# The P V product of a thresholded attention in four 64x64 tiles and two phases, and the ninth-token blocks transposed by two 64-row transfers

## The chip, the core and the metric

One Trainium2 chip, of which one core is used. The metric is the device time of one execution in microseconds (us); the median of 3 runs of the kernel before is 466.98 us (466.92 to 468.55).

## What is computed

Batch 8, 8 heads, 576 tokens, head dimension 64; then a feed-forward layer of 512 to 768 to 512 on the 8 x 576 tokens. All inputs and the output are float32.

```python
scores = scale * np.matmul(q, k.transpose(0, 1, 3, 2))
thresh = np.max(scores, axis=-1, keepdims=True) - tau
scores = np.where(scores >= thresh, scores, -1000000000.0)
attn = np.exp(scores - np.max(scores, axis=-1, keepdims=True))
attn = attn / (np.sum(attn, axis=-1, keepdims=True) + 1e-09)
attn_out = np.matmul(attn, v)                      # P V
x = attn_out.transpose(0, 2, 1, 3).reshape(B * S, H * D)
h = np.maximum(np.maximum(x @ w1, x @ w2), x @ w3)
out = h @ w_out
```

## The kernel before

**Units.** Four heads of a batch make a quad; there are 16 quads, two for each batch. In a quad, heads 2r and 2r+1 form pair r, and inside a pair the head is i. A token sits at partition p, column c of nine (token = 9p + c), so the 576 tokens of a head are eight blocks of 64 tokens that go in couples of 128, and a ninth block of 64. A chunk is 128 query rows by the 576 keys of one head for each of the two pairs: nine chunks for each quad. Chunk index 4 (`idx == 4`) is the ninth-token block: its first 64 partitions belong to head i = 0 and its last 64 to head i = 1.

**Stages of a chunk.** `scores` (S) makes four float32 matmuls of 64 contraction rows for one r; `maximum` (m) is on VectorE; `exponents` (e) on ScalarE; `numerators` (n on ScalarE, k on VectorE); `reciprocals` (r) on VectorE; `normalized` (p) on GpSimd writes P, 128 x 1152 in bf16; `turned` (t) has SyncE (SP) issue one DMA transpose of P into the quad's tile `ptq`, 128 keys x 9 blocks x 1152 queries.

**The product** (`product`, letter O). For one quad and one r, the output tile `o` holds head i on partitions 64i to 64i+63 and the 576 queries along the free side, in two PSUM banks of 512 and 64 columns. Five steps m accumulate: m = 0 to 3 are four couples of 128 keys, with weights `vb`; m = 4 is the ninth block, with weights `vrb`. The ninth block's 64 keys of pair r lie on partitions 64r to 64r+63 only, so `vrb` is 128 partitions tall and zero elsewhere (six memsets at the start, and `cast_v` fills it in two copies of 64 partitions). Each step is, for the 512 columns and then for the 64, one matmul for each i: 128 contraction rows by 64 output columns of the array, which the trace writes as form `128*64`. That is 20 matmuls and 20 weight loads for each product. `on_scalar` (x) and `on_vector` (w) copy `o` into `xt`: for r = 0 VectorE takes all 576 columns, for r = 1 ScalarE takes 512 and VectorE 64.

**The last batch** (b = 7) is worked in two parts: queries of four couples (256 for each head), then the remaining 320. A product of part 1 is ten matmuls of 256 columns, one of part 2 is ten of 256 and ten of 64. So there are 28 whole products and 8 of parts, 680 matmuls.

**Feed-forward.** `ffn` makes pieces: hidden (`ph`, letter F) and output (`po`). They use `halves`: the contraction of 128 is split over the two 64-row halves of the array (form `64*128`), each half accumulating into its own bank; the letter B issues the second phase, in which the halves swap banks. Ahead of the second phase stands a `tensor.nop()` that waits for the last matmul of the first.

**Order.** The string `ORDER` fixes the order of issue on every engine; each letter makes one step, and `_Ordered` chains each engine's instructions in that order (so nearly every line of the profile is L89). A digit behind S, T, O or F is the PSUM slot, of which there are four of two banks each. T is the transposition of q or k on TensorE (`tp`); l issues loads on SP, y is `cast_v` on GpSimd, o issues stores on SP. PE, SP and GpSimd take their work strictly in that order; there is no other scheduling.

The tile pools that matter: `pt` has 2 buffers, `pp` (P) 6.

Of the kernel before, what the change touches and what calls it, by code (L numbers as in the profile page):

```python
# [12 lines left out]
BF16 = mybir.dt.bfloat16  # L13
AX = mybir.AxisListType.X
AF = bass_rust.ActivationFunctionType
# [22 lines left out]
ORDER = """  # L38
lllS0lmyS1eyS2lmlS3kelmnS0lmegS1repmgS2kyemnS3pT0meS1tmeymaS3S2knS0llremplekT3pnlrS1meqmnpmteprceT2qketS3pS0
anT1rmS2lpnmS3qlempntrcS2pekT1eptS0mnqmelprkalS3petS1mnS2qrmnS0lperlmpetkpeT3mnlS1pmetS2mpnremptekyS0nS2qmlT  # L40
1nzrcaemT1pS3ekpteS0mnS2yrmqelcplnS3rplnmS1tpemS2epmS0tepmS1nrS3mptekpT0erlekO2qtamnpS0melpmleS1kteT3rmnpS0l
nqmleprwnS1qeS2pmtnS0mpeO1czntrmnpS3wekT0permT2aptkeS0pxS3rcnS1gpmtnS2rpmepmetS0mqnO3qmegprnS2wynS0mS1etprmO
3epkeztxS2mewmpF3egS0kpeS2rnBmzF1tmhnkyS3egS2rpmBeF0pnvpBtemF1nkT3zBevF2akS0pghBmnF3tS1rvepBmnpS2F0rveqtS1mp
BmS3ezremF2pghkS1zetBmnF0vS3epgBnmF2pS1vetBmT0hS3rcpeF1S2rmpBmpteF0vpeBknS3ztF1nmS2vyeT3gzBmlO0hrlpalnpF1wle
T3ytBcnS0kS2nlmzO3nlrmeqlvelS2pS0rwxrmyF1npmS3gqBekqeF2vntpBmnS0pS1hmpgeS2mpeS3rmpeF0tmpeBrnS1pvS2tepmF0nzS3
metBrmpT2nS1vpaS3tnS0zmS2ermtpF1nkpnmS3eByrtmepkepF2lemlukS0utkBermnpoT1rekpoS0ecO3lupmtnpO1weoqurktpnS3T0xr
wS2mapoF1meT3qlS0cetBqmF3phS2kleqBmlF1nyF0lrnvBelpBrvS3yhpS2mnF1ptmS0epBmeF2ptvnF3BkeS1tvBnS0mhF2rmepS3rBepm
S1nytvF0peS3mpBnlmS2yetvT3eF1maS0lkBeqlS3mhlF2rmeplT1nlcpS0eBlrmpF1tnS3kpeBmnlO0qvernvtpT2S3wapS1nrmF2ptnS0m
qBempF3hS1kqteO2meykT0rxrBwpceS2yvnS0ylmF1nlS3pmelF2pmtBeBkpeS0vhlS3nrtmF1pS2mepBrlmeF3ptS0vepS2mnBtmF1evnT2
lS0kuS3lakS1onF2rmpemlepS0rkepBtmnpmF3erqktepT1uBuconqroS0yuS2pumoS1pT3mteS0ympeO2koayntmO3ewqelrkS1qxlT2wS0  # L50
rnmlpF3mlepcS1BleyF0tmphS2kpeBlmF3nF1lyveBtrknBpS0vhS2lpnrmF3S1pmetBpmeS0veS1tF2mnS3meBlmnF1F0lveBrelkpS2lBh
mF3npF1vBetkS0nrrBvpF2mhpS3BeptmS1nyvT0T3nrmO2parcyetpS0ewqS3mnO1pmeptkeS2qT3xwS0mayF1meqF3kBeqBrnvT2pS0hclS
1ynmtF3nS2mpBelmpF1elS0vetBmnF3rS2veplBmnpF1S0rhkptBemF3nprS2vleBpmS0tnpvF1emS3tuS2rkepS1nrF0mopnmepS3tmeS2p
rmBeptmeykS1yelS2mupS3lumO1temekT0oeF2ronwplakT3nT1qcS0nBpmnqtraS3peO1mqukuqonT0wS3rocpxS2lmeF0ptrF1mepBkpS3
thBremS0plvF2eptS3mS1ymeBlmF0pelS3veBmF2thS1keBknF0lmF3nlBveBlrknF2plS1rhvBnpmF3nS0pvtBepmF2rS1vtepBmpF0hT3k
tBerS2pavS1npF3mS0qmteBrmepO2vnpeS1twnS3mS0nF2meS1meBrmF0phS3knpBemO2eqvterkpT1xT0wS3caF2pnmT1qBtnrcF0pnvS3q
lBempF1lhS2rkyleBtmF0pvS3epBlrnmS1ypnvF2pterS3mpuS0meS2ptF1meymetS3knS0keBomnrmS2eplS3umpF0luroemptS2ekpT1em
T3oBakteqcT1nS2klaS3rmulpO1umoqeorkyeS0S2npmO3nprtwepmS1xpT0wtnmF2qS3ecpBlermF0qlhkS1pteBmnF2S3pvleBymlnF1vS
0eBtnmF2hS3keBlrmpF1nlvF0pnBlrpS2etvBynmS3S1hlrpmF2erpS0mteBpmeS3pvtnF0S1myeyF2pmeBktBeF3khT1vBaS2vnT0qS1rmp
O3meqcepS2wnF0tS1rnmpT3nmBpS2arvpS1temF3qeO0mpeketT2kxBnwS1clF0hrlmS2pnlBrkyeF3lmF1BrveqlBkpnF0lS2vhlBprmT3t  # L60
S1pvaS2pmeF0tS3mpeBkpteF1vnS2pmulS0moS1eF3metrmepS2knpS1S0nmBertmpekpS1nF2mertmpeS0kepS1mBuuqmtnS0keO3omeoku
O1urkoperowT2xpwT0cS3aqtS1nmF2qrF0myepBekS3yBhmF1pnS2vqteBmpnT0F3rcpelS2vBpnlS0mtphS1meS3mteF2knBmleS0lrnvpS
1ermF2plnS3pmteBpmF1eS0rveptBmnpF2kS3htBemF1nS0rvpleBmpF2nlrS3vpelT0mBtpaS1khS3qtmS0eqO2nmekerS3mpS1nmpO0ewt
ermpF2xwT3kpeF0cnBF1ntvT3BnkBarvS2phT3rrF0mqS1pceBmqtT3nS2pvS1ampS0eF3mpteF2mqeBkByeT1vhS0cT3pS2amF1qtnmF3qe
BkqBevS0nrF2vpT1rmupS3noS2cpnS0mpF1etmyeyrmpS2etkBepmnS3ktuS0urmF2peompnorS1kpeS3tmeS0BpmemteS1kuS0urS3kopnO
2ormepeO1pmnpweO0twrxmO2pxkS1eptS0xmnF3mS2teBkF0hmF1nBkS3ervF2peBmpBveS0ytF3hmS1F2emBkF0eBrvnpBrF1vphS3kpBtF
2mF0pveBytS3nyvO1kO2xrmF1xpBrkepS2BhmF3nptF0vepBF1ntvBS2hBmF3vS0eBrmpF1F2vpeBnS3thS0mBmF1eS3veBmnF0vO2urkepo
O1S0xpS3mF1tmekS0eBmweF3rkpnkuS2pnBorrmupteF0pF1hF2nopvF0tuvpF1rhF2pvF0tvF1phF2vF0tvF1hF2uvF0ovF3hoF1vF2vF0h
F3vF1vO2uoO0wF3xF1F2hF0vF1vF2hF0vF1vF2hF0vF1vF2hF0vF1vF2hF0vF1vF2hF0vBvF1uuooBF2uuouoo
"""  # L70


# [28 lines left out]
def kernel(  # L101
# [23 lines left out]
    tensor, scalar, vector, pool, sync = (  # L125
        _Ordered(tc, e) for e in (nc.tensor, nc.scalar, nc.vector, nc.gpsimd, nc.sync))
    B, H, S, D = q.shape
# [8 lines left out]
    one = ctx.enter_context(tc.tile_pool(name="one", bufs=1))  # L136
# [40 lines left out]
    def bank(name, where):  # L177
        return ps_s.tile([128, 1024], F32, name=name, tag=f"s{where}")
# [35 lines left out]
            yield  # L214


    vrs = [one.tile([128, 4, D], BF16, name=f"vr{x}") for x in range(3)]

    def cast_v(L):
        L["vb"] = vp.tile([128, 4, 4, D], BF16, name="vb")  # L220
        pool.tensor_copy(out=L["vb"], in_=L["vm"])
        yield
        L["vrb"] = vrs[(2 * L["b"] + L["qd"]) % 3]
        for r in range(2):
            rows = slice(64 * r, 64 * r + 64)
            pool.tensor_copy(out=L["vrb"][rows, 2 * r:2 * r + 2], in_=L["vr"][rows])
            yield

    def couple(L, n, r, j, rows=slice(0, 128)):

# [121 lines left out]
    def turned(c):  # L352
        L = Ls[c["g"]]
        if "pt" not in L:
            L["pt"] = pt_pool.tile([128, 9, W], BF16, name="ptq")
        sync.dma_start_transpose(out=L["pt"][:, :, c["idx"] * 128:(c["idx"] + 1) * 128], in_=c["P"])

    def product(L, r, target, part=None):

        pt, vb, vrb = L["pt"], L["vb"], L["vrb"]  # L360
        st = {}

        runs = {None: ((0, 640, 0, 512), (512, 576, 512, 64)),
                1: ((0, 640, 0, 256),),
                2: ((256, 896, 0, 256), (512, 576, 256, 64))}[part]

        order = [(m, run) for m in range(5) for run in runs] if part is None else \
            [(m, run) for run in runs for m in range(5)]

        def first(where):  # L370
            st["ps"] = ps = bank("o", where)
            for m, (*q0, p0, n) in order:
                for i in range(2):
                    w = vb[:, 2 * r + i, (1, 3, 0, 2)[m], :] if m < 4 else vrb[:, 2 * r + i, :]
                    tensor.matmul(ps[64 * i:64 * i + 64, p0:p0 + n], w,
                                  pt[:, 4 if m == 4 else m + 5 * r, q0[i]:q0[i] + n],
                                  start=(m == 0), stop=(m == 4))

        def on_vector():
            ps = st["ps"]  # L380
            dst = target(L["b"])[:, 2 * L["qd"] + r, :]
            if part is None and r == 0:
                vector.tensor_copy(out=dst, in_=ps[:, 0:S])
            elif part is None:
                vector.tensor_copy(out=dst[:, 512:S], in_=ps[:, 512:S])
            else:
                vector.tensor_copy(out=dst[:, 256:S], in_=ps[:, 0:320])

        def on_scalar():
            ps = st["ps"]  # L390
            dst = target(L["b"])[:, 2 * L["qd"] + r, :]
            if part is None:
                scalar.activation(out=dst[:, 0:512], in_=ps[:, 0:512], func=AF.Copy)
            elif part == 1:
                scalar.activation(out=dst[:, 0:256], in_=ps[:, 0:256], func=AF.Copy)
            else:
                scalar.activation(out=dst[:, 256:S], in_=ps[:, 0:320], func=AF.Copy)
        p = _Piece((L["b"], L["qd"], r, part), first)
        p.vector = on_vector if part is None or part == 2 and r == 0 else None
        p.scalar = on_scalar if part == 1 or r == 1 else None  # L400
        return p
# [137 lines left out]
        return hTs[b]  # L539

    wl = list(weight_loads())
    for t in vrs:
        for x in range(2):
            vector.memset(t[64 - 64 * x:128 - 64 * x, 2 * x:2 * x + 2, :], 0.0)
    warm = bank("warm", 3)
    for _ in range(WARM):
        tensor.transpose(warm[:, 0:128], identf, identf)
# [2 lines left out]
    for x, (r, n) in enumerate(((0, "q"), (0, "k"), (1, "q"), (1, "k"))):  # L550
        p = transposed(Ls[0], n, r)
# [30 lines left out]
        while True:  # L582
            yield from fn(line[what].pop(0))

    made, pending = [], []
    todo = dict(S=((c, r) for c in chunks() for r in range(2)),
                T=((g, n, r) for g in range(1, NQ) for r in range(2) for n in "qk"),
                O=products(), F=pieces())
# [7 lines left out]
    def issue(what, where):  # L596
        if what == "S":
            c, r = next(todo["S"])
            c[r] = scores(Ls[c["g"]], c["idx"], r, where)
            line["m"].append((c, r))  # L600
        elif what == "T":
            g, n, r = next(todo["T"])
            p = transposed(Ls[g], n, r)
            p.first(where)
            line["a" if n == "q" else "c"].append((p, g, r))
        elif what == "O":
            p = next(todo["O"])
            p.first(where)
            for k, fn in (("x", p.scalar), ("w", p.vector)):
                if fn:  # L610
                    line[k].append(fn)
        elif what == "F":
            p = next(todo["F"])
# [5 lines left out]
        elif what == "B":  # L619
            p = pending.pop(0)  # L620
            p.second()
            line[p.kind].extend(p.done)
        elif what == "m":
            c, r = line["m"].pop(0)
            c["bias", r] = maximum(c, r)
            line["e"].append((c, r))
        elif what == "e":
            c, r = line["e"].pop(0)
# [71 lines left out]
```

## Time and profile before

| | us |
|---|---|
| median of 3 runs | 466.98 (466.92 to 468.55) |
| the profiled execution, first to last instruction (span) | 465.6 |
| median less span | 1.4 |
| PE busy (matmuls) | 437.9 (94%) |
| VectorE, ScalarE, GpSimd busy | 403.9 (87%), 394.0 (85%), 318.7 (68%) |
| PE busy on the P V product | 47.2, in 680 matmuls |
| mean granted TensorE clock | 0.970 |

The page gives no time of its own for the profiled execution beside the span; the 1.4 us between span and median lie around the program's instructions. Busy time of PE counts a matmul to its modelled end, so a PE that is 94% busy still has room between matmuls. The chain is followed back from the last instruction, and its shares say what set the end. A form such as `64*128 64x288` reads: 64 contraction rows by 128 output columns of the array are used, and the moving operand is 64 partitions x 288 columns.

The 36 products in the order of the program, with their start in the trace of before, and the letters that PE sees around them after the change (P is the new letter; digits left out):

| no. | start, us | PE's letters from its O on | no. | start, us | PE's letters |
|---|---|---|---|---|---|
| 1 | 49.78 | O S P S | 17 | 259.11 | O S P S |
| 2 | 59.20 | O S P T | 18 | 265.23 | O T P T |
| 3 | 66.82 | O S P S | 19 | 286.99 | O S P S |
| 4 | 69.89 | O P S | 20 | 289.52 | O P S |
| 5 | 98.15 | O F P T | 21 | 310.74 | O S P F |
| 6 | 101.80 | O S P S | 22 | 316.13 | O T P B |
| 7, 8 | 123.97 | O O P P S | 23, 24 | 338.08 | O O P P T |
| 9 | 149.58 | O T P S | 25 | 362.54 | O S P S |
| 10 | 154.81 | O T P B | 26 | 365.06 | O P F |
| 11, 12 | 176.80 | O O P P S | 27, 28 | 393.73 | O O P P O |
| 13 | 200.04 | O S P S | 29, 30 (part 1) | behind 28 | O P, O P S |
| 14 | 208.31 | O S P T | 31, 32 (part 1) | 411.51 | O O P P F |
| 15 | 231.03 | O T P F | 33, 34 (part 2) | 425.37 | O O S P P S |
| 16 | 237.08 | O T P S | 35, 36 (part 2) | 442.93 | O O P P F |

### The profile page before, as it was taken

The numbers are of one execution on the slowest core, as the hardware profiler recorded it, in microseconds if no ns is written. First come the engines' busy times: TensorE is split into PE (matmuls) and PEld (weight loads), VectorE is DVE, ScalarE is ACT, GpSimd is POOL, SyncE is SP. The second block draws the span as 40 slices with busy tenths as digits, with TensorE's granted clock in tenths as the row PEclk, the third lists the DMA queues.
The fourth block names the chain that finished last, engine by engine and source line by source line (L and its number), as shares of the span: only waits on it lengthen the run. The fifth ranks groups of instructions, "written<-read, shape, count | busy, mean of one in ns | idle before, by whom it ended". The sixth has DMA issues, their size and how long they took to land.

```text
span 465.6 us, 14101 instructions
## 1 busy us (share of the span) xinstructions
PE 437.9 (94%) x5188; PEld 314.1 (67%) x5188; DVE 403.9 (87%) x1115; ACT 394.0 (85%) x794; POOL 318.7 (68%) x416
## 2 busy tenths in 40 slices
PE   7778788999999999979999999999999999999995
PEld 5444545666686777648678676877776777787872
DVE  3987899889999989949999899999999999887641
ACT  3998999789999998849988999988999989866622
POOL 3699788699878878556685687767776597462500
PEclk8995899999999999979999999999999999999999
DMA  8999999799999999996999699999979949654702
GB/s 256 242 210 232 199 222 246 166 237 275 216 232 183 212 161 230 221 215 135 207 214 229 130 189 212 212 196 220 160 190 224 153 84 223 105 102 66 173 32 103
DMA packets 212773, 87.44 MB, mean 188 GB/s; under 512 B 185824, under 2 KB 199648, under 8 KB 212704
## 3 DMA queue, kind: packets, MB, share of 16 engines
q1 hardware_dynamic: 212144, 85.95, 89.6%
q8 instruction: 41, 0.67, 0.6%
q10 hardware_dynamic: 560, 0.59, 0.5%
q14 instruction: 28, 0.23, 0.1%
HBM read 34.60 MB, written 9.44 MB: 95 GB/s over the span
## 4 chain that ended last, share of the span: by engine, by line
PE 70%; DVE 11%; ACT 11%; issue 5%; DMA 2%; POOL 0%; SPq 0%; ACTq 0%; DVEq 0%; POOLq 0%
PE sc L89 25%; PE ph L89 25%; ACT z L89 9%; PE po L89 8%; PE o L89 8%; DVE z L89 6%; PE tp L89 3%; DVE unused L89 2%; DMA ptq<-P 1%; DMA qm<-in_q_dram 1%; DVE kt L89 1%; DVE hT L89 1%; ACT xt L89 1%; ACT hm L89 1%; DVE hm L89 1%
## 5 line engine op out<-in xcount | busy, mean ns | idle before, releaser
L89 POOL TENSOR_SCALAR P<-z,rs 128x576 bf16<-128x576 f32 x288 | 229.5, 810 | 94.7 <-DVE rs L89 58.5
L89 PE MATMUL sc<-kt,qt 64*128 64x320 f32 (+2 forms) x640 | 192.7, 442 | 4.2 <-ACT z L89 2.2
L89 PE MATMUL sc<-kt,qs 64*128 64x256 f32 (+2 forms) x640 | 189.7, 431 | 6.2 <-ACT z L89 4.1
L89 PE MATMUL ph<-xt,w 64*128 64x288 bf16 (+2 forms) x2160 | 170.9, 283 | 1.2 <-DVE xt L89 0.3
L89 PEld LDWEIGHTS <-w 64*128 64x128 bf16 (+1 forms) x2160 | 125.0, 94 | 41.1 <-issue 12.6
L89 ACT ACTIVATE z<-sc,nm 128x576 f32<-128x576 f32 x179 | 129.9, 739 | 21.1 <-DVE unused L89 15.5
L89 DVE TENSOR_SCALAR_CACHE_REDUCE unused<-sc 128x576 bf16<-128x576 f32 x179 | 132.2, 749 | 8.2 <-PE sc L89 7.0
L89 ACT ACTIVATE z<-z 128x576 f32<-128x576 f32 x179 | 121.3, 680 | 0.3
L89 PEld LDWEIGHTS sc<-kt,qs 64*128 64x128 f32 (+1 forms) x640 | 93.2, 182 | 27.3 <-ACT z L89 7.4
L89 PEld LDWEIGHTS sc<-kt,qt 64*128 64x128 f32 (+1 forms) x640 | 93.1, 182 | 18.2 <-ACT z L89 6.7
L89 DVE SCALAR_TENSOR_TENSOR z<-z 128x576 f32<-128x576 f32 x109 | 93.3, 861 | 1.0 <-ACT z L89 0.9
L89 DVE TENSOR_SCALAR_CACHE_REDUCE z<-sc 128x576 f32<-128x576 f32 x109 | 81.1, 750 | 11.7 <-PE sc L89 9.9
L89 ACT ACTIVATE z<-z,nm 128x576 f32<-128x576 f32 x109 | 82.0, 771 | 9.8 <-DVE z L89 9.7
L89 POOL COPY qs<-qt 64x640 f32<-64x640 f32 (+1 forms) x62 | 46.9, 756 | 21.8 <-ACT qt L89 18.6
L89 PE MATMUL po<-wo,hT 64*128 64x512 bf16 (+1 forms) x480 | 54.2, 356 | 0.1
L89 ACT ACTIVATE hm<-ph 128x576 bf16<-128x576 f32 (+2 forms) x54 | 32.1, 595 | 16.2 <-PE ph L89 15.9
L89 DVE TENSOR_TENSOR hm<-ph,hm 128x576 bf16<-128x576 f32 (+2 forms) x54 | 36.9, 684 | 9.9 <-PE ph L89 9.1
L89 PE MATMUL o<-ptq,vb 128*64 128x64 bf16 (+2 forms) x544 | 40.6, 288 | 3.4 <-DMA ptq<-P 3.1
L89 PEld LDWEIGHTS <-hT 64*128 64x128 bf16 (+1 forms) x480 | 30.2, 97 | 17.6 <-issue 3.9
L89 DVE TENSOR_TENSOR hT<-ph,hm 128x576 bf16<-128x576 f32 (+2 forms) x54 | 37.0, 685 | 2.9 <-PE ph L89 1.4
L89 PEld LDWEIGHTS <-vb 128*64 128x64 bf16 x544 | 22.9, 113 | 20.9 <-issue 8.5
L89 ACT ACTIVATION_READ_ACCUMULATOR z<-z 128x1 f32 x179 | 35.4, 198 | 0.0
(32 smaller groups left out, 279.9 us busy)
## 6 DMA issues: line engine op xcount, KB each, us to landing
vm<-in_v_dram SPq DMA_DIRECT2D x32, 256.0 KB, 4.4
out_dram<-ob SPq DMA_DIRECT2D x32, 256.0 KB, 2.7
qm<-in_q_dram SPq DMA_DIRECT2D x15, 512.0 KB, 4.4
km<-in_k_dram SPq DMA_DIRECT2D x15, 512.0 KB, 5.5
stage<-in_moe_w_dram SPq DMA_DIRECT2D x9, 512.0 KB, 4.5
ptq<-P SPq DMA_TRANSPOSE x144, 3.9
stage<-in_moe_w_out_dram SPq DMA_DIRECT2D x3, 512.0 KB, 5.9
qm<-in_q_dram SPq DMA_DIRECT2D x16, 64.0 KB, 2.4
```

What stands on the lines that cost most here:

```text
L89: ins = fn(*a, **kw)
```

## The change

The product uses the array as four tiles of 64x64: the contraction of 128 keys is split into halves h (form `64*64`), and each half accumulates half of the queries into its own bank. In phase 0 half h works on bank 1 - h; in phase 1, behind a `tensor.nop()` that waits for the last matmul of phase 0, the banks are swapped. A whole product is 2 phases of 18 matmuls of 288 columns: four for each of m = 0 to 3, and for m = 4 the two of the half h = r, where the ninth block's keys lie. Parts have 2 x 18 matmuls of 128 or 160 columns. Phase 0 stays at the letter O; phase 1 is issued by a new letter P, of which 36 are put into `ORDER`. Nothing else of `ORDER` is altered. Copies out of `o` keep their engines and sizes, as 2 x 288, 2 x 256 and 2 x 32 columns.

The transposition of chunk 4 becomes two DMA transposes of 64 rows of P, so that each head's 576 queries lie side by side in `ptq`. `vrb` has no zeros left: the six memsets are gone, and `cast_v` fills it with one copy of 128 partitions in place of two of 64.

```diff
-1nzrcaemT1pS3ekpteS0mnS2yrmqelcplnS3rplnmS1tpemS2epmS0tepmS1nrS3mptekpT0erlekO2qtamnpS0melpmleS1kteT3rmnpS0l
+1nzrcaemT1pS3ekpteS0mnS2yrmqelcplnS3rplnmS1tpemS2epmS0tepmS1nrS3mptekpT0erlekO2qtamnpS0PmelpmleS1kteT3rmnpS0
...
-    vrs = [one.tile([128, 4, D], BF16, name=f"vr{x}") for x in range(3)]
+    vrs = [one.tile([128, 2, D], BF16, name=f"vr{x}") for x in range(3)]
...
-        for r in range(2):
-            rows = slice(64 * r, 64 * r + 64)
-            pool.tensor_copy(out=L["vrb"][rows, 2 * r:2 * r + 2], in_=L["vr"][rows])
-            yield
+        pool.tensor_copy(out=L["vrb"], in_=L["vr"])
+        yield
+        yield
...
-        sync.dma_start_transpose(out=L["pt"][:, :, c["idx"] * 128:(c["idx"] + 1) * 128], in_=c["P"])
+        x = c["idx"]
+        for i in range(2) if x == 4 else (None,):
+            rows = slice(0, 128) if i is None else slice(64 * i, 64 * i + 64)
+            at = 128 * x - 64 * (x > 4) if i is None else S * i + 512
+            sync.dma_start_transpose(out=L["pt"][:, :, at:at + rows.stop - rows.start], in_=c["P"][rows])
...
-        runs = {None: ((0, 640, 0, 512), (512, 576, 512, 64)),
-                1: ((0, 640, 0, 256),),
-                2: ((256, 896, 0, 256), (512, 576, 256, 64))}[part]
...
+        pt, vb, vr = L["pt"], L["vb"], L["vrb"]
+        t0, n = {None: (0, S // 2), 1: (0, 128), 2: (256, 160)}[part]
+
+        def phase(swap):
+            ps = st["ps"]
+            if swap:
+                gate = tensor.nop()
+                tc.add_manual_dep(gate.ins, st["last"], ...)
+            for m in range(5):
+                for i in range(2):
+                    for h in (1, 0):
+                        if m == 4 and h != r:
+                            continue
+                        rows = slice(64 * h, 64 * h + 64)
+                        w = vb[rows, 2 * r + i, (1, 3, 0, 2)[m], :] if m < 4 else vr[rows, i, :]
+                        last = (3, 4)[h == r]
+                        a = (1 - h) ^ swap
+                        cols = S * i + t0 + a * n
+                        ins = tensor.matmul(ps[64 * i:64 * i + 64, 512 * a:512 * a + n], w,
+                                            pt[rows, 4 if m == 4 else m + 5 * r, cols:cols + n],
+                                            start=(not swap and m == 0), stop=(swap == 1 and m == last))
+            st["last"] = ins.ins.name
...
-                    tensor.matmul(ps[64 * i:64 * i + 64, p0:p0 + n], w,
-                                  pt[:, 4 if m == 4 else m + 5 * r, q0[i]:q0[i] + n],
-                                  start=(m == 0), stop=(m == 4))
...
-    for t in vrs:
-        for x in range(2):
-            vector.memset(t[64 - 64 * x:128 - 64 * x, 2 * x:2 * x + 2, :], 0.0)
...
             p = next(todo["O"])
             p.first(where)
+            waiting.append(p)
+        elif what == "P":
+            p = waiting.pop(0)
+            p.second()
             for k, fn in (("x", p.scalar), ("w", p.vector)):
```

## The prediction

> **What bounds the kernel now.** I read the page's busy times and its chain first, then the timeline of PE around products, and then SP's timeline and the ptq transfers.
>
> ```profile
> PE 437.9 (94%) x5188; PEld 314.1 (67%) x5188; DVE 403.9 (87%) x1115; ACT 394.0 (85%) x794; POOL 318.7 (68%) x416
> ...
> PE 70%; DVE 11%; ACT 11%; issue 5%; DMA 2%; POOL 0%; SPq 0%; ACTq 0%; DVEq 0%; POOLq 0%
> ```
>
> PE carries 70% of the chain, so what a product costs PE is mostly paid in full. The chain between 66 and 72 us shows how: product 3, three chunks' scores, product 4, with no wait.
>
> ```profile
> 66.89 1.36 PE o L89 x20
> 68.25 1.71 PE sc L89 x12
> 69.95 1.38 PE o L89 x20
> ```
>
> Asked in this way around every product, the chain runs through all but 1, 6, 7, 8, 11, 12 and 26. The timeline of PE at product 3 (start, length of the group, last the count; a length includes the end of the pipeline):
>
> ```profile
> 66.46 0.43 PE L89 MATMUL sc<-kt,qs 64*128 64x320 f32 x1
> 66.82 1.18 PE L89 MATMUL o<-ptq,vb 128*64 128x512 bf16 x16
> 67.83 0.41 PE L89 MATMUL o<-ptq,vr 128*64 128x512 bf16 x4
> 68.18 0.48 PE L89 MATMUL sc<-kt,qs 64*128 64x256 f32 x1
> 68.18 0.53 PE L89 MATMUL sc<-kt,qt 64*128 64x320 f32 x1
> 68.50 0.38 PE L89 MATMUL sc<-kt,qs 64*128 64x256 f32 x1
> 68.56 0.43 PE L89 MATMUL sc<-kt,qt 64*128 64x320 f32 x1
> 68.71 0.43 PE L89 MATMUL sc<-kt,qs 64*128 64x320 f32 x1
> ```
>
> Steps m begin 0.247 us apart in the trace, so 5 steps stream in 1.235 us: the product already runs at the pace of its columns. Around it lies what a change of form costs. A 320-column score takes 0.27 us of streaming (that is the distance of two in one half), so 66.46 + 0.27 = 66.73, and the product starts at 66.82: 0.09. At the way out it is again 0.09, and the first score then blocks its half until 68.50, 0.32 us where the next takes 0.21: 0.10 more, for a weight load that nothing hides. The same reading gives 0.02 for a product's own first step, 0.05 in front of `tp` and 0.01 in front of `ph`.
>
> **Part 1, four tiles instead of two: nothing gained in streaming.** Form `64*64` exists in the scores of chunk 4:
>
> ```profile
> 88.65 0.53 PE L89 MATMUL ph<-xt,w 64*128 64x288 bf16 x5
> 89.11 0.43 PE L89 MATMUL sc<-kt,qs 64*64 64x256 f32 x2
> 89.12 0.49 PE L89 MATMUL sc<-kt,qt 64*64 64x320 f32 x2
> 89.37 0.38 PE L89 MATMUL sc<-kt,qs 64*64 64x256 f32 x2
> 89.44 0.44 PE L89 MATMUL sc<-kt,qt 64*64 64x320 f32 x2
> 89.81 0.42 PE L89 MATMUL ph<-xt,w 64*128 64x288 bf16 x4
> ```
>
> All four tiles start within 0.02 us and run together; and the form is entered and left at the same 0.09 (last 320 score at 89.45 + 0.27 = 89.72, `ph` at 89.81). The 288-column `ph` steps follow each other every 0.1225 us (24 pairs take 2.94 us in the chain). A whole product is ten such rounds, five in each phase (m = 4 fills two tiles of four but lasts as long): 10 x 0.1225 = 1.225, against 1.235. Times 28: -0.3 us.
>
> **Part 2, the second visit.** Where another letter stands between O and P, the array changes form twice more. Behind S: 0.09 + 0.10 + 0.09 + 0.02 = 0.31 us, ten times (1, 2, 3, 6, 13, 14, 17, 19, 21, 25). Behind T: 0.09 + 0.05 + 0.09 + 0.02 = 0.25, six times (9, 10, 15, 16, 18, 22). Behind F: 0.21, once (5). Together 4.8; less 0.6 for 1 and 6, which are off the chain: +4.2 us. Pairs O O P P pay nothing, as the other product's phase covers the wait at the swap.
>
> Where P follows its O directly (4, 20, 26, and 29 and 30 of the parts), the nop waits for the end of phase 0, and everything behind it on PE is queued. `ph` shows the price when its two phases meet:
>
> ```profile
> 76.68 0.47 PEld L89 LDWEIGHTS <-w 64*128 64x128 bf16 x8
> 77.52 0.73 PEld L89 LDWEIGHTS <-w 64*128 64x128 bf16 x14 [0.37 <-PE ph L89]
> ```
>
> The trace has the two matmuls around this gap 0.344 us apart where 0.122 is the pace: 0.22 for each. 26 is off the chain; the other four give +0.9. The pair 33, 34 (O O S P P) pays 0.3.
>
> **Part 3, the last batch's parts.** 128 and 160 columns stream in 0.056 and 0.069 us, so a round may be set by the start of four matmuls instead. The nearest row is product 35's 64-column run, ten matmuls, of which the next begins 0.155 us after the first:
>
> ```profile
> 443.47 0.29 PE L89 MATMUL o<-ptq,vb 128*64 128x64 bf16 x8
> ```
>
> That is 0.0155 each, 0.062 for four: ten rounds 0.62 against 5 x 0.109 = 0.545 in part 1, and 0.69 against 5 x 0.137 = 0.685 in part 2; four of each, +0.3 us. The farther row, 20 `tp` matmuls in 0.62 us, gives 0.124 for a round, 1.12 for a product (its two half rounds at 0.06) and +4.0 in all. I take +0.3, the row of the same operation, and keep 4.0 for the range.
>
> The Trainium skill (TensorE: Matmul & The Clock Gate, Part 1, "Wait — 56ns, not 53.3ns?") puts a floor of about 25 ns under the distance of two matmul starts. By it a round of four could not be under 0.10 us, and the parts would cost, as an estimate from that figure, +2.3 in place of +0.3: 476. The trace speaks against it as a floor of the whole array: 15.5 ns at 443.47.
>
> **Part 4, what waits for the later product.** Phase 1 ends behind the letter between, so ScalarE's or VectorE's copy starts later by that letter's own work too (S 0.54, T 0.31). Where the chain goes through the copy, this counts: product 2, where VectorE waits for it (+0.55), and 10, whose copies free the bank for the next scores (+0.3). Elsewhere PE's next work covers it: +0.9 in all.
>
> **Part 5, the transposes.** 16 more issues on SP. A transfer's two ends: two halves may issue in the time of one (nothing), or each at the price of a whole one:
>
> ```profile
> L89 SPq DMA_TRANSPOSE ptq<-P x144: 1242/1352/3633, 15.5 to 438.9; - x144
> ```
>
> so 0 to 1.24 us. Plain DMAs of 64 partitions (`obr`, 0.57) and of 128 (`ob`, 0.58) issue alike, so about 0.5 of the 1.35 looks fixed: I take 0.5. Behind the pair on SP stand loads, stores and the quad's later transposes. Between chunk 4's transfer and the last one SP has no gap in the quads of products 1, 7, 9, 13, 17, 21 and 35; from the last landing to the product the trace has 6.7, 3.6, 3.6, -3.5, 0.7, 0.0 and 0.7 us. So 0.5 is paid at 13 and 21, +1.0, and hidden by that slack elsewhere; at 1.24 it would be 3.6. Product 13 is the one that already waits: the trace has PE idle for 3.1 us until ptq has landed, at 203.50, and the granted clock (behind the x counts of PE, PEld, VectorE, ScalarE and GpSimd) then stands at 0.50:
>
> ```profile
> 202.57:209.40 6.83, 5.85 (x37) 3.41 (x39) 2.40 (x6) 0.98 (x4) 2.04 (x4) 0.50 0.97 218
> ```
>
>
> **Part 6, removed.** GpSimd loses 16 copies of 0.39 us, at 68% busy and almost never on the chain: 0 to -1, I take -0.4. VectorE's six memsets (0.7 us) lie beside the first load of q, 1.7 to 7.0 us in the chain: nothing; without that cover 0.7.
>
> **Sum.** -0.3 + 4.2 + 0.9 + 0.3 + 0.3 + 0.9 + 1.0 - 0.4 = +6.9 us. Span 465.6 + 6.9 = 472.5; the median stood 1.4 above the span: **474 us**. About 0.5%, 2.3 us, is what a measurement can tell here.
>
> **Rivals.** *The wait at product 13 swallows it.* If the landing at 203.50 is set by SP and the DMA queues (SP is busy without a gap from 183 to 201 us) and not by PE, the 2.4 us that PE comes later by then (products 2, 3, 4, 5, 9, 10, part 4) are spent inside its 3.5 us wait; with about 1 us of idling left, the clock may not fall, which saves the 2.9 us that 5.85 us at half clock cost: 474 - 2.4 - 2.9 = 468.8, not slower by what can be told. It decides if less than about 2.5 us of waiting is left, as the clock fell 2.5 us into it. Against: the stretch starts from stores and P's that hang on PE's own work, and so move with it. 0.16.
>
> *The copies come late everywhere.* If each of the 17 separated products pays the letter between as well, in VectorE or in banks freed late: 10 x 0.54 + 7 x 0.4 - 0.9 = +7, 481 us. For: 14 copies already wait for `o`, 10.9 us. Against: behind most products the chain stays on PE. 0.14.
>
> *SP's tail:* whole price for a half transfer, 2.6 more, 476.6; inside the forecast's own range. With the tp pace in the parts too: 480. 0.10.
>
> *The four tiles don't run together* (bf16 unlike the scores): rounds of 0.245, 28 x 1.2 = +34, 508 us. 0.03.
>
> *Faster:* GpSimd's copies out of the way and scores that come 0.5 us sooner behind a half-long O, at all 17, if VectorE and ScalarE set those places: the 4.2 is hidden and up to 8.5 gained, 461 to 470. The chain says PE. 0.07.
>
> **Numbers.** The forecast's own case, 470 to 478, has 0.50. The range from 467.5 to 482 takes in the swallowed wait and the late copies, and leaves out faster, 508, and a tail of either. Faster 0.07; same 0.13 (most of the swallowed wait); slower 0.80.
>
> **What would show it.** Right: `o` 1296 matmuls in form `64*64`, rounds 0.1225 us apart, 0.25 to 0.31 us more of PE for each separated product, streaming unchanged; SP's half transfers near 0.9 us. Wrong: rounds of another pace; a change of form that costs other than 0.09; the wait at product 13 gone or grown; idle time in front of `xt` well above 10.9 + 5 us.

## The result, and the profile after

The changed kernel takes **480.11 us** (median of 4 runs, 477.72 to 482.37), the kernel before beside it on the same chip 467.76 (466.92 to 470.27): a ratio of **1.0265 (1.0215 to 1.0316)**, 12.4 us slower. The forecast was 474, 7 us slower, with a range from 467.5 to 482. The side was right and the range holds the time; the sum was 5.4 us short.

The profiled execution has a span of 477.3 us, 11.7 over before. Its busy times and its chain, by engine and by line:

```profile
PE 441.4 (92%) x5804; PEld 316.3 (66%) x5804; DVE 398.9 (84%) x1109; ACT 394.1 (83%) x794; POOL 312.8 (66%) x400
...
PE 58%; DVE 13%; ACT 11%; issue 7%; DMA 6%; POOL 3%; SPq 1%; ACTq 0%; DVEq 0%; POOLq 0%
PE sc L90 21%; PE ph L90 20%; ACT z L90 9%; PE o L90 8%; PE po L90 7%; DVE z L90 6%; DMA ptq<-P 5%; DVE unused L90 3%; PE tp L90 3%; POOL P L90 2%; DVE kt L90 1%; DMA qm<-in_q_dram 1%; SPq L90 1%; DVE hm L90 1%; ACT xt L90 1%
```

PE is busy for 3.5 us more but has only 58% of the chain where it had 70%; DMA went from 2 to 6%, nearly all of it `ptq<-P`, the transposes of P. So much of the loss is not work on PE but PE waiting. The groups of the tile ptq say for what (the row of its transfers: minimum, median and maximum ns of an issue on SP; below, what ended PE's idle time before a product, and from issue to landing):

```profile
L90 SPq DMA_TRANSPOSE ptq<-P x160: 1200/1340/4124, 15.3 to 451.4; - x160
...
  DMA ptq<-P: 7.9, 7
...
DMA to landing us min/median/max: 2.7/4.0/8.5
```

Before it was 3.1 us, once, at product 13. Now it is 7.9 us in seven places, of which the largest, 2.2 us in two pieces, is a new one at product 3. The chain there (start, length, what):

```profile
62.31 1.49 POOL P L90 x3
63.79 4.16 DMA ptq<-P
67.95 0.04 issue
67.99 1.35 PE o L90 x14
69.34 1.36 PE sc L90 x4
```

These rows answer to the three of product 3 before, which followed each other without a wait. Here the last transpose of the group lands at 67.95, 1.25 us later than before (66.70). PE had begun product 3 at 64.99, stood still for 1.8 and 0.45 us, and the granted clock (behind the x counts) then was 0.50:

```profile
66.63:73.46 6.83, 5.92 (x44) 3.57 (x46) 1.37 (x4) 2.15 (x6) 3.48 (x5) 0.50 1.16 237
```

The 14 matmuls that are left take 1.35 us, and products and scores up to 73 run at half speed. Before, the only such stretch behind a wait of a product was at product 13 (202.6 to 209.4). There the changed kernel has none: PE comes later, waits 2.1 us in place of 3.1, and keeps its clock.

Where the time is lost can be read from the starts of the products in the two traces (after less before, us): product 1 -1.2, 3 -1.8, **4 +4.0**, 9 +3.9, 13 +5.3, **14 +2.7**, 17 +3.2, **18 +5.8**, 21 +6.6, **22 +8.5**, 27 +9.3, 35 +10.9, end +11.7. The steps in bold are the waits for ptq at 3, 17 and 21, and the one that got shorter at 13; between them the difference grows slowly. The steps are what to read here, and not the level at the start: two traces of one kernel (e7 and e7b below) already differ by 3.7 us at product 1.

### The profile page after: what moved, and what is told of

It is laid out like the page before. It is cut to its first block, busy times and chain, and to the rows that moved or that the text cites. A ratio compares the mean times of both kernels' runs of the same rounds, so it can differ in the third digit from the quotient of the medians.

```text
span 477.3 us, 15309 instructions
## 1 busy us (share of the span) xinstructions
PE 441.4 (92%) x5804; PEld 316.3 (66%) x5804; DVE 398.9 (84%) x1109; ACT 394.1 (83%) x794; POOL 312.8 (66%) x400
## 4 chain that ended last, share of the span: by engine, by line
PE 58%; DVE 13%; ACT 11%; issue 7%; DMA 6%; POOL 3%; SPq 1%; ACTq 0%; DVEq 0%; POOLq 0%
PE sc L90 21%; PE ph L90 20%; ACT z L90 9%; PE o L90 8%; PE po L90 7%; DVE z L90 6%; DMA ptq<-P 5%; DVE unused L90 3%; PE tp L90 3%; POOL P L90 2%; DVE kt L90 1%; DMA qm<-in_q_dram 1%; SPq L90 1%; DVE hm L90 1%; ACT xt L90 1%
## 5 line engine op out<-in xcount | busy, mean ns | idle before, releaser
L90 PEld LDWEIGHTS sc<-kt,qs 64*128 64x128 f32 (+1 forms) x640 | 90.9, 179 | 26.8 <-ACT z L90 8.1
L90 PEld LDWEIGHTS sc<-kt,qt 64*128 64x128 f32 (+1 forms) x640 | 90.7, 179 | 21.9 <-ACT z L90 7.3
L90 DVE SCALAR_TENSOR_TENSOR z<-z 128x576 f32<-128x576 f32 x109 | 88.9, 820 | 0.2
L90 PE MATMUL o<-ptq,vb 64*64 64x288 bf16 (+2 forms) x1152 | 46.8, 278 | 9.6 <-DMA ptq<-P 7.9
L90 PEld LDWEIGHTS <-vb 64*64 64x64 bf16 x1152 | 29.8, 107 | 28.3 <-issue 20.5
L90 DVE CAST xt<-o 128x576 bf16<-128x576 f32 (+2 forms) x30 | 14.5, 488 | 29.0 <-PE o L90 22.9
```

The lines of the kernel that those rows point to most:

```text
L90: ins = fn(*a, **kw)
```

## The experiments

All times are medians; each ratio is to runs of the kernel before on the same chip. Loads, stores and transposes of P are all issued by SP, one after the other.

**Each half of the change alone (e1, e2).** e1 is the kernel before with chunk 4 of P in two transfers to the same columns:

```diff
-        sync.dma_start_transpose(out=L["pt"][:, :, c["idx"] * 128:(c["idx"] + 1) * 128], in_=c["P"])
+        x = c["idx"]
+        for i in range(2) if x == 4 else (None,):
+            rows = slice(0, 128) if i is None else slice(64 * i, 64 * i + 64)
+            at = 128 * x + (0 if i is None else 64 * i)
+            sync.dma_start_transpose(out=L["pt"][:, :, at:at + rows.stop - rows.start], in_=c["P"][rows])
```

> The kernel before with one part of the change alone: chunk 4 transposed by two 64-row transfers into the same columns as before. Theory A (SP's price): a half transfer issues as long as a whole one (1.20 to 1.28 us in the trace of after, against 1.24 at least for a whole one), so SP pays 1.25 us more for each quad, and where a quad's last transfer has no room before its product PE waits: 4.5 to 6.5 us over before (1.0 to 1.4%). Theory B (the product's price): the split costs only what the prediction took for it, 1 to 2 us (0.2 to 0.4%), and the rest of the measured 12 us is in the product's second visit and its late copies.

Measured: 475.32 us, 1.0165 (1.0132 to 1.0197), by the ratio 7.7 us slower. More than theory A had, and far from B. The timeline of SP has the two halves of one chunk (x2), and the tile ptq the idle time of PE that it ended (us, times):

```profile
53.13 2.57 SPq L89 DMA_TRANSPOSE ptq<-P  x2
```

```profile
  DMA ptq<-P: 7.0, 4
  issue: 4.9, 1
```

A half takes 1.25 us of SP (median 1.245 and 1.269 of the first and second ones), where a whole transfer takes 1.35. So a split costs SP nearly a whole issue. The product that pays most is 3, which had 0.12 us to spare before. Its wait of 4.9 us is the one that the profile puts down to "issue": PE starts again at 69.84, and the last transpose of the group landed at 69.75, so it belongs to the waits for ptq as well, 11.9 us in all.

e2 is the changed kernel with one transfer of 128 rows for chunk 4:

```diff
-        x = c["idx"]
-        for i in range(2) if x == 4 else (None,):
-            ...
+        sync.dma_start_transpose(out=L["pt"][:, :, c["idx"] * 128:(c["idx"] + 1) * 128], in_=c["P"])
...
-                        cols = S * i + t0 + a * n
+                        cols = ({None: 576, 1: 640, 2: 832}[part] if i else t0) + a * n
```

> The changed kernel with chunk 4 transposed by one transfer of 128 rows, as before; the product keeps its four tiles and two phases, and reads head 1's queries from their old columns, so they come out in another order (the work and its amount are the same, the output isn't the reference's). Theory A: what is left is the product's own price, 5.5 to 7.5 us over before (1.2 to 1.6%), and PE's wait for ptq falls back from 7.9 us to about 3. Theory B: 10 us or more (over 2.1%), as the second visits and the late copies carry nearly all.

Measured: 473.84 us, 1.0141 (1.0095 to 1.0186), 6.5 us slower, as theory A had it; its waits for ptq are 2.7 us. They are not the old one: 2.0 are at product 21, and at product 13 only 0.5 is left, without half clock behind it. The two halves of the change add up to 3.1%, the whole is 2.65%: they overlap a little, since a product that comes later waits less.

**The same split by columns (e3).** The kernel before, chunk 4 as 128 rows x 640 and 128 rows x 512 columns.

```diff
+        for f0, f1 in ((0, 5), (5, 9)) if x == 4 else ((0, 9),):
+            sync.dma_start_transpose(out=L["pt"][:, f0:f1, x * 128:(x + 1) * 128], in_=c["P"][:, 128 * f0:128 * f1])
```

> The kernel before with chunk 4 transposed by two transfers that halve the columns of P in place of its rows: 128 rows by 640 and by 512. It asks what an issue's time goes by. If by a fixed price for each issue: 1.2 us for each again, and the time of the split by rows. If by the number of column blocks (nine of 128 in a whole one, and nine in each 64-row half): about 0.7 and 0.6 us, SP loses almost nothing, and the time is that of before within 0.4%. If by rows times columns, the two splits would both have halved it, which the trace of after already excludes.

Measured: 476.57 us, 1.0214 (1.0161 to 1.0267), with 6.6 us of waits for ptq in four places and 4.2 us at product 3 under "issue", as in e1. The parts take 1.25 and 1.26 us of SP. So a half has the same price whichever way P is cut; it isn't the 64 rows.

**The second phase directly behind the first (e4).** e2 with every P of ORDER moved to its O, so that nothing stands between and the copies of `o` into `xt` start as early as they can.

> As the one with four tiles and one transfer (so the output isn't the reference's, as there), but with every P directly behind its O: no second change of form, in its place the wait at the swap, and copies that can start sooner. By the prediction's prices the 17 separated products go from 0.31 or 0.25 to 0.22 to 0.25 us and the four pairs O O P P from nothing to 0.25 for each product: about the same on PE (within 1.5 us of that kernel), and 0.9 us less for the late copies. If late copies are what costs (rival), 4 us or more faster than that kernel; if PE's queue standing at the nop costs more than the row of ph shows, slower by 2 us or more.

Measured: 473.72 us, 1.0153 (1.01 to 1.0206), not to be told from e2; the 4 us less of the rival did not come. This doesn't show that the place of the second phase makes no difference, for the two traces lose their time in different places. PE in e4 is ahead of e2 by 1.6 us at product 1 and by 5.1 at product 13. There it waits, and e2 hardly does (first e4, then e2, then e4's clock):

```profile
201.20 1.16 PE L90 MATMUL o<-ptq,vb 64*64 64x288 bf16 x13 [2.73 <-DMA ptq<-P]
```

```profile
204.03 0.68 PE L90 MATMUL o<-ptq,vb 64*64 64x288 bf16 x13 [0.48 <-DMA ptq<-P]
```

```profile
200.16:206.99 6.83, 5.73 (x57) 3.55 (x59) 2.07 (x4) 1.33 (x3) 2.18 (x3) 0.50 1.11 183
```

Product 14 starts only 0.7 us ahead. Between such waits, from product 7 to 13 and from 14 to 21, e4 loses 0.3 and 0.4 us on the kernel before, e2 1.3 and 1.8; from 22 to the end e4 loses 3.7 and e2 2.9. Nor did all copies come early: the idle time of VectorE and ScalarE in front of `xt` until a product is done is 10.9 us before, 32.5 in the changed kernel, 22.8 in e2 and still 19.6 in e4.

**Larger transfers (e5).** If the price were fixed, fewer and larger transfers would be the cure: two chunks of P in one tile and one transfer, 80 in all.

```diff
-PBUFS = 6
+PBUFS = 3
...
-            L["pt"] = pt_pool.tile([128, 9, W], BF16, name="ptq")
-        sync.dma_start_transpose(out=L["pt"][:, :, c["idx"] * 128:(c["idx"] + 1) * 128], in_=c["P"])
+            L["pt"] = pt_pool.tile([128, 9, 9, 128], BF16, name="ptq")
+        ...
+        sync.dma_start_transpose(out=L["pt"][:, x + 1 - n:x + 1].rearrange("p x m c -> p (x m) c"),
+                                 in_=c["pair"][:, 0:n].rearrange("p x w -> p (x w)"))
```

> The kernel before, with two chunks of P transposed by one transfer of 128 rows x 2304 columns where before there are two of 1152 (chunks 0+1, 2+3, 4+5, 6+7, then 8 alone; 84 transfers in place of 144). Theory A, the price of a transfer on SyncE is fixed (1.2 us whatever its size, as the halves by rows and by columns showed): the pairs take 1.3 to 1.6 us each, SyncE is relieved of some 5 us in each group of four heads, the wait for ptq at product 13 (3.1 us) and the half clock behind it go, and the time falls by 2 to 5 us, to 462 to 465. Theory B, the price goes with the bytes (the halves were at a floor that the whole one is over): a pair takes 2.4 us or more, nothing is saved, and the time is within 1.5 us of the kernel before. A third outcome, slower by 2 us or more, if the three buffers of pairs, which hold no more than the six single ones, make GpSimd wait for P.

(The count in that text should read 80, 64 pairs and 16 single ones.) Measured: 477.69 us, 1.0179 (1.0112 to 1.0246). The transfers of the tile ptq, and from the list of waits what GpSimd lost (in total, times, longest):

```profile
L91 SPq DMA_TRANSPOSE ptq<-P x80: 1254/2897/7277, 20.2 to 449.2; - x80
```

```profile
POOL P L91 <- DMA ptq<-P: 18.1, 7, 4.5
```

Theory B and the third outcome together. A pair takes 2.5 us of SP at the least and 3.2 in the median; the single ones of the same run take 1.25 at the least and 1.34. So the price is not fixed: half a chunk costs nearly as much as one, but two cost at least twice as much. And with three buffers of pairs GpSimd waits for a free one. The cure is not this.

**The split where there is time (e6).** e1, but only in the seven groups whose products came 3.6 to 6.7 us after their last transpose had landed.

```diff
+SPARE = (0, 2, 3, 4, 5, 9, 13)
...
-        for i in range(2) if x == 4 else (None,):
+        for i in range(2) if x == 4 and c["g"] in SPARE else (None,):
```

> The kernel before with the two 64-row transfers of chunk 4 in 7 of the 16 groups alone: those whose first product before began 3.6 to 6.7 us after its last transpose had landed (products 1, 5, 7, 9, 11, 19, 27). Theory A, the extra transfer costs only where the product already waits for its transposes: within 1.5 us of the kernel before (465.8 to 468.8). Theory B, each extra transfer costs its part wherever it stands (the split in all 16 groups cost 7.7 us): 7/16 of that, 3 to 4 us, so 470.5 to 471.5.

Measured: 469.46 us, 1.0017 (0.9992 to 1.0041). Theory A: seven of the sixteen extra transfers cost nothing that can be told, at most 1.9 us by the interval, so most or all of the 7.7 us of e1 comes from the other nine.

**SP relieved (e7, e9, e10, e11).** Four kernels with the same edit of ORDER: the loads of later groups (`l`) that stand among the last five transposes of a group are moved behind the last one. For one group:

```diff
-O3ewqelrkS1qxlT2wS0rnmlpF3mlepcS1BleyF0tmphS2kpeBlmF3nF1lyveBtrknBpS0vhS2lpnrmF3S1pmetBpmeS0veS1tF2mnS3meBlmnF1
+O3ewqerkS1qxT2wS0rnmpF3mepcS1BeyF0tmphS2kpeBmF3nF1yveBtrknBpS0vhS2pnrmF3S1pmetBpmeS0veS1tllllllllF2mnS3meBlmnF1
```

e7 is the kernel before with it, and e9 the changed kernel.

> The kernel before with its loads of later groups (q, k, v; letters l of ORDER) that stand on SyncE among the last five transposes of a group moved behind the last one, where their first reader is at least 35 letters away (59 loads in 12 groups; 8 of them, some 6 us of SyncE, in the group of product 13). Theory A, SyncE's queue is what makes the transposes land late: the wait for ptq at product 13 goes (3.1 us) and the half clock behind it too (6.8 us at half speed, of which up to 3.4 are lost), and the time falls by 2 to 5 us. Theory B, the transposes are late because P is (GpSimd) or because of the transfers themselves: within 1 us of the kernel before.

> The changed kernel with the same 59 loads moved behind the last transpose of their group. Theory A, of its 12.4 us over the kernel before some 6 are late transposes behind SyncE and some 6.5 the products themselves: the waits for ptq (7.9 us, 7 times) fall below 3 us, and the time falls by 4 to 6 us, to 474 to 476. Theory B, the waits for ptq are set by something else than SyncE's queue: within 1.5 us of 480.

(The loads moved are 67, not 59.)

e7: 467.84 us, 0.9977 (0.9948 to 1.0007). No matmul of a product waits for ptq any more, yet nothing is gained. e9: 476.79 us, 1.0199 (1.0149 to 1.0249), waits for ptq 0.7 us; 3.3 us less than the changed kernel by the medians, less than theory A had. Both leave the same question, why a wait of 3.1 us with half clock behind it is worth nothing when it goes. The next two put the halves of the change on this order, and the third took e7 again beside them.

> The kernel before with the loads moved as in e7 and every chunk 4 transposed by two 64-row transfers as in e1. Theory A, the extra transfers cost only where a product waits for its transposes, and behind the moved loads none does: no waits of PE for ptq over 1 us in all, and within 1.5 us of e7 (467.8). Theory B, they cost something else too: 3 us or more over e7, as e1 cost 7.7 over the kernel before.

> The four-tile products with one 128-row transfer of each chunk 4 (as in e2) and the loads moved as in e7: the price of the products alone, with no transposes late in either kernel. If the second visits, the swap waits and the parts cost what the terms of the sum said (4.2 + 0.9 + 0.3 + 0.3 - 0.3 = 5.4): 472.5 to 474.5. Rival, the products cost more than their own stretches on PE (copies of o into xt start later, and with them the scores of later groups): 475.5 to 477.5, as e9 with its split transfers took (476.8). As in e2, head 1's queries stand in another order, so that the output isn't the reference's.

> The kernel of e7 again, beside e10 and e11 on one chip, with more rounds. If taking the wait for ptq at product 13 away is worth the wait and the half clock behind it: 2 to 5 us below the kernel before. If something else comes late in its place: within 1 us of it, as e7's ratio of 0.9977 (0.9948 to 1.0007) had it.

e10, the split: 471.27 us, 1.0062 (1.0026 to 1.0097), 2.9 over e7's 468.39 of this series, with 0.2 us of waits for ptq; between the two theories, close to B's 3, and far below the 7.7 of e1. e11, the four tiles: 475.44 us, 1.0176 (1.013 to 1.0222), 7 us over e7, between the two theories. e7 again: 468.39 us, 1.0 (0.9968 to 1.0031). The timeline of PE in front of product 9 answers the question; first e7, then e10 (start, length, count, and in brackets the idle time before it and what ended it):

```profile
144.87 0.52 PE L89 MATMUL tp<-identf,qm 64*128 64x64 f32 x10 [2.40 <-DMA qm<-in_q_dram]
```

```profile
147.24 0.80 PE L89 MATMUL tp<-identf,qm 64*128 64x64 f32 x10 [3.53 <-DMA qm<-in_q_dram]
```

Five of the moved loads were wanted soon: the transposes `tp` of the group behind wait for their q, and the clock falls to a half for 3.4 us in e7 and 6.8 in e10. It is a new wait, and takes back most of what was gained: against the kernel before, e7 loses 3.9 us from product 7 to 9 and e7b 4.2, and between products 13 and 14 each gains 5.7. From product 9 to 33 e10's products start a constant 3.6 us later than e7's, and a constant 1.5 us earlier than those of e7b, the second trace of e7's kernel. So the eleven extra transfers behind that place add nothing. What lies before it can't be read as finely, as e7 and e7b are themselves 3.7 us apart at product 1 and 4.7 at product 7; but from product 7 to 9 e10 loses 2.3 us more than e7 and 2.0 more than e7b, which is most of the 2.9. That its q comes later because SP has more to issue is likely, but not shown.

**All but those five (e12).** e7 with the loads of the group of product 9 left where they were.

> The kernel of e7 with the loads of the group of product 9 left where they were before: 54 moved in place of 59. e7's profile has no wait for ptq, but at 142.5 us a new one of 2.4 us, the transposes tp of the group behind waiting for the q that came later, and a stretch of half clock behind it. Theory A, this new wait is what took back what the wait at product 13 gave: it goes, and the time falls to 463 to 465.5, 0.6 to 1.2 per cent below the kernel before. Theory B, something else comes late as soon as PE gets ahead: within 1 us of e7 and of the kernel before (467 to 469).

(By the right count, 62 loads in place of 67.)

Measured: **462.58 us, 0.9883 (0.9859 to 0.9908)**. Theory A; it beats both kernels. The page's busy times and granted clock, and 14 us around product 13 (start and end, length, then busy time and count of PE, PEld, VectorE, ScalarE and GpSimd, the granted clock, DMA):

```profile
PE 432.1 (94%) x5188; PEld 309.1 (67%) x5188; DVE 404.0 (88%) x1115; ACT 394.2 (86%) x794; POOL 320.5 (70%) x416
...
PEclk9989999999999999999999999999999999999998
```

```profile
198.00:212.00 14.00, 13.88 (x189) 10.87 (x187) 12.67 (x33) 13.10 (x27) 11.97 (x17) 1.00 1.03 222
```

The same 14 us before held 108 matmuls at a clock of 0.76. From product 7 to 13 the kernel before is 0.2 to 0.3 us ahead of e12, and from 15 to the end 5.5 to 5.9 us behind: the gain is made at this one wait. Between the starts of products 13 and 14 it is 5.67 us, and the same 5.67 in e7, e7b and e10.

## Why the prediction was right and where it fell short

**Parts 1 and 3, four tiles: right.** `o` takes 52.75 us of PE (47.2 before) in 1296 matmuls:

```profile
0.00:478.00 478.00, 52.75 (x1296) 14.55 (x30) 10.54 (x20) 0.98 0.90 183
```

Rounds are 0.1225 us apart, as forecast, and the four tiles run together; the rival of 508 us is out. In the parts, two products of 128 columns have this timeline of PE:

```profile
421.55 0.42 PE L90 MATMUL o<-ptq,vb 64*64 64x128 bf16 x16
421.80 0.22 PE L90 MATMUL o<-ptq,vr 64*64 64x128 bf16 x2
422.03 0.42 PE L90 MATMUL o<-ptq,vb 64*64 64x128 bf16 x16
```

From the first start to the last row's last start, 72 matmuls take 1.27 us: 0.64 for a product where the forecast had 0.62, and the 1.12 of the `tp` row is out. But that 0.64 is so near is in part luck. Inside a phase rounds of four follow each other every 0.056 us, which is the pace of 128 columns and not four starts of 0.0155; the rest is mainly one gap of 0.23 us between the first two phases, which the forecast did not have. The floor of about 25 ns under two starts that the Trainium skill states (TensorE: Matmul & The Clock Gate, Part 1, "Wait — 56ns, not 53.3ns?") doesn't hold for four tiles together: 32 matmuls begin 13.8 ns apart here.

**Part 2, changes of form and swaps: right where it could be read.** At full clock, and where nothing is waited for, every change of form into and out of `64*64` takes 0.09 us (88 to 95 ns). In product 4, with P directly behind its O, the last of 36 matmuls starts 1.384 us after the first where 1.135 would do without the swap: 0.25 against 0.22.

**Part 4, later copies: right in kind, too small.** The products alone cost 7 us by the medians (e11 against e7b, 475.44 and 468.39) and 8 by the ratios, where Parts 1 to 4 and 6 came to 5.9; with some 2.5 us of uncertainty either way these alone don't set the sum and the measured price apart. The traces do: from product 9 to 22 e11 falls 4.7 us behind e7 (and e7b), where the forecast's terms for these products add up to 3.3. The steps from product to product agree where the chain stays on PE (13 and 14: 0.35 and 0.37, forecast 0.31 each), are larger at 9, 10, 17, 18 and 21 (0.74, 0.79, 0.68, 0.71, 0.99, forecast 0.25 to 0.55), and smaller at 15, 16 and 20 (0.14, -0.07, -0.28, forecast 0.25, 0.25, 0.22). The chain of e11 at product 10:

```profile
163.29 0.46 PE tp L90 x8
163.75 0.75 PE o L90 x18
164.50 0.02 issue
164.53 0.61 ACT xt L90
165.13 0.02 issue
165.15 0.24 DVE xt L90
```

The letter T between the phases, the second phase, the copies on ScalarE and VectorE, and behind them, from 165.53 on, the next scores, which need the bank. The forecast had named this for product 10, at 0.3; in e7 the chain at this place runs on VectorE alone up to the scores. That the letter between is a loss for the copies fits e4's smaller steps from 7 to 13 and from 14 to 21. How much of it would be left for a kernel without waits for ptq is open: no run has P directly behind O together with the moved loads.

**Part 5, the transposes: this is the step that failed.** It took e = 0.5 us for an extra issue, from plain DMAs of 64 and 128 partitions, and put it on products 13 and 21: +1.0. A half transfer takes 1.25 us, so e is near the upper bound of 1.24; the plain DMAs were the wrong row, and the sign that the forecast named, halves near 0.9 us, did not come. But even the bound gave only 3.6, and the split alone costs 7.7. The other part of the miss is the list of products: it went by gaps of SP. The group of product 3 has one of 0.5 us (in the trace of before from 55.8 to 56.3 us), so that product is not on the list, though it started 0.12 us after the landing. And it charged the delay alone, not the half clock behind the wait, which the forecast itself had priced at 2.9 us for product 13. e6 shows that the slack was the right measure, and e12 what a wait is worth with its clock: 5.7 us between products 13 and 14 for 3.1 us of idling, near to 3.1 + 2.9. Product 3 shows the same sum. Its landing came 1.25 us later, with 0.12 to spare; 1.1, 2.9 and the 0.3 of its own second visit make 4.3, and product 4 starts 4.0 us later than before.

The clock by itself: each stretch at 0.50 that ends within a span lasts 3.413, 6.827 or 10.240 us, that is once, twice or three times 3.413. The Trainium skill (TensorE: Matmul & The Clock Gate, Part 1: The HAM clock gate) states windows of 3413 ns that run freely, and half rate after at least one idle window of that length. The traces agree in the length of the stretches, but not in the waiting that brings them: 1.7 us at product 21 of e4 and 2.4 in e7 were enough for one window, and 2.7 in e4, 3.1 before and 3.5 in e10 brought two, while 2.8 us at product 13 of e5 brought none, nor did the changed kernel's 2.1 there, and the 4.7 us of e1 brought only one. So a wait may cost a half clock behind it, and its length alone doesn't say whether.

And on the split: the Trainium skill (DMA: Bandwidth & Descriptors, Rules for kernel authors) advises against two transfers to two halves of the partitions in place of one. e1 agrees, with 1.65%, and e6 shows the limit: 0.17% where the product is not waiting.

**The rivals.** *The wait at product 13 swallows it* came true at 13 (in e2 almost whole, 4.5 us between products 13 and 14) and was outbid elsewhere: the wait there shrank and the half clock behind it went (product 14 starts 2.6 us less late than 13), but product 3 got both. *The copies come late everywhere* read the profile right, with 32.5 us of idle time in front of `xt` against its mark of 10.9 + 5, though part of it is PE's own waiting for ptq. Its price, 7 us on top of the sum, is denied by e11: the products alone would cost some 13 us, and cost 7 to 8. *SP's tail* had the right price for a half transfer and too few places for it.

So the 12.4 us are about 7 of products, where the forecast had 5.9, and some 5 of late transposes, of which it had 1. That the range held is in part luck: its upper end was there for late copies, and late transposes with half clock filled it.

## What to carry to other kernels

Before an instruction is added to a queue, list for every consumer how long after the landing it starts; the queue's own gaps say less, and a consumer with 0.1 us to spare pays everything. Price a wait of the matmul engine with the half clock that may follow it, and look for both in the trace even of a kernel that is not to be changed: here moving 62 loads behind transposes took one such wait away and gained 1.2%. When a wait goes and the time stays, look for the new one in the same trace before concluding that it was free.

## What the runs showed of the hardware

A DMA transpose of bf16 within SBUF occupies SP's queue, in the median, for 1.25 us at 64 x 1152 as at 128 x 640 and 128 x 512, 1.35 us at 128 x 1152 and 3.2 us (2.5 at the least) at 128 x 2304: below one chunk it hardly falls with size, above it at least doubles. Plain DMAs of the same queue take 0.4 to 0.65 us in the median, by what they move.
